# Block sums of a mixing matrix: added by VectorE and GpSimd, or by transfers in DRAM

## The chip, the cores and the metric

One core of a Trainium2 chip runs the whole program. The time is that of the device for one execution, in microseconds (us), and the median over several executions is compared. The engines that matter: TensorE (PE in the profile; PEld is its weight load) multiplies, VectorE (DVE) and GpSimd (POOL) do element-wise work, ScalarE (ACT) does activations and copies out of PSUM, SyncE (SP) only issues transfers. ScalarE and GpSimd issue transfers too. Each engine takes its instructions in order.

## The reference

The input x is 2048 x 512. It is normalised by rows (xn), and two branches are made of it:

```python
xn = _layernorm(x, axis=-1)
s = _A_ref(xn, A_wqkv, A_wo)      # attention: 32 heads of 16, 8 taps at distance 2, then @ wo
g = _silu(_B_ref(xn, B_w_in, B_w_sp, B_b_sp, B_w_out))
return x + s * g

def _B_ref(x, w_in, w_sp, b_sp, w_out):
    z = _gelu(jnp.einsum("bsd,df->bsf", x, w_in))     # 2048 x 1792
    z1 = z[..., :Fh]                                  # Fh = 896
    z2 = _layernorm(z[..., Fh:], axis=-1)
    g = jnp.einsum("ts,bsf->btf", w_sp, z2) + b_sp[None, :, None]
    return jnp.einsum("bsf,fd->bsd", z1 * g, w_out)
```

The mixing weights w_sp are 2048 x 2048 in float32.

## The kernel before

**Number format.** Every matrix operand is split into a high and a low part (`split`, lines 194 to 198: ScalarE writes the high part, VectorE subtracts it for the low part), and each product is three matmuls: high by high, high by low, low by high. `prep` (line 175) loads a block of weights into one of four raw buffers (`fetch`, line 167, on SP's queue) and splits it into one of eight weight pairs.

**Stages on TensorE, in order:** the projections q, k, v (`product`, `pair`, three groups g of 16 row tiles, written to DRAM as `qkv_d`); z1 (seven blocks f by four column groups c, lines 695 to 711, written to DRAM as `z1_d`); z2 (eight pairs of row tiles i and 8 + i, lines 780 to 801); the mixing product w_sp by z2 (`block_product`, from line 990); the projection by w_out (`proj`, line 1075); and the projection by wo (line 1124).

**The mixing by fewer products.** w_sp is cut into column halves a = 0, 1 and within each into four kinds of block: t0, t1 (rows' upper half r = 0, columns c = 0, 1) and l0, l1 (lower half). A Strassen-like scheme uses the plain blocks and four sums of them:

- number 0: t0 + t1 + l1
- number 1: t0 + t1
- number 2: l0 + t0 + t1 + l1
- number 3: t1 + l1

There are 16 sets, for a = 0, 1 and i = 0 to 7; each block of a set is 128 x 512. `added` (line 390) makes the four sums of one set in four adds. `block_sums` (line 395) loads the four blocks by two transfers of 512 KB, adds, and stores by two transfers to `sums_d`. The sets (a = 1, i = 0 to 5) run on GpSimd, loads, adds and stores alike (`pool_sums`, called at line 488 in the q, k, v stage). The eight sets of a = 0 run on VectorE during z1 (`first_sums`, lines 690 to 715; loads on SP, stores on GpSimd's queue, tiles from the eight buffers `t4` that z1's and z2's results use too). The last two sets run on VectorE during z2 (`raw_sums`, line 405, in the raw buffers of the weights, loads and stores on SP in transfers of 256 KB). `summed` (line 872) loads the sums for the later block products.

**z2 to mixing.** For each pair i VectorE takes statistics (`z2_stats`, line 738; line 745 adds epsilon), GpSimd raises to the power -0.5 (line 746), ScalarE normalises (line 754), the result is split and combined (`combine`, line 759). The first mixing products need these and the weight blocks `wsp_*`. The PSUM banks are first seeded with the biases by ScalarE (`seed`, line 842).

**Attention** is VectorE work, put between the rest: 32 steps (16 units by two), each with a product of q and k (line 573), its reduction to scores (580), a weighted product of the values (620), a fold on GpSimd (633), two more folds and a transpose (638 to 646), and a store. They are kept in one order by `line` (537), have a low priority (`LOW`) except for the score reductions, and are placed where a planner's model of the times finds VectorE free. `sums_of` lists the 32 weighted products. One hold is set by hand: the tenth weighted product (`sums_of[9]`) comes behind the split of block wsp_6 of the first mixing product (lines 864 to 867). It is an order on VectorE, not a semaphore.

Of the kernel before, what the change touches and what calls it, by code (L numbers as in the profile page):

```python
# [57 lines left out]
def kernel(  # L58
# [40 lines left out]
    y_d = dram.tile([2, ODD, P, CT], F32, name="y_d")  # L99
    sums_d = dram.tile([2, 2, HT, P, 2, CT], F32, name="sums_d")  # L100
    t_d = dram.tile([3, HT, P, F3], F32, name="t_d")
# [287 lines left out]

    def added(ts, eng):  # L390
        t0, t1, l0, l1 = ts
        for out_, p_, q_ in ((l1, t1, l1), (t1, t0, t1), (t0, t0, l1), (l0, t0, l0)):
            eng.tensor_tensor(out_, p_, q_, op=ALU.add)  # L393

    def block_sums(a, i, tile_=None, eng=nc.vector, loads=nc.sync, stores=nc.scalar, behind=None):
        top, low = [(tile_ or t4)(f"s{n}_{a}_{i}") for n in "ab"]
        for t, r in ((top, 0), (low, HT)):
            ins = loads.dma_start(t, w_sp[2 * a : 2 * a + 2, r + i].rearrange("c p t -> p c t"))
            if behind:
                tc.add_manual_dep(ins.ins, behind[0].ins.name, behind[1], reason="sums later")  # L400
        added([top[:, 0], top[:, 1], low[:, 0], low[:, 1]], eng)
        for r, t in enumerate((top, low)):
            stores.dma_start(sums_d[a, r, i], t)

    def raw_sums(a, i):
        ts = [
            fetch(w_sp[2 * a + c, r + i], CT, f"sr_{a}_{i}_{c}_{r}") for r in (0, HT) for c in range(2)
        ]
        added(ts, nc.vector)
        for n, t in enumerate(ts):  # L410
            nc.sync.dma_start(sums_d[a, n // 2, i, :, n % 2], t)

    def early_tile(name):
        return t2(name).rearrange("p (i t) -> p i t", i=2)

    def pool_sums(a, i, tile_, *behind):
        block_sums(a, i, tile_, nc.gpsimd, nc.gpsimd, nc.gpsimd, behind)

    z1_sums = [(0, i) for i in range(HT)]

# [57 lines left out]
    for j in range(11, NT):  # L478
        if j + 2 < NT:
            fetch_cols(j + 2)  # L480
        if j == NT - 3:
            rb = raws.tile([P, 512], F32, tag="raw", name="rb", bufs=RAW)
            rbv = rb.rearrange("p (j q) -> p j q", j=JC)
            pin(nc.sync.dma_start(rbv, mv_d[:JC, 1].unsqueeze(0).to_broadcast([P, JC, P])))
        turned = column_tile(j)
        if j == 12:
            for i in range(HT - 2):
                pool_sums(1, i, early_tile, turned, SYNC)
        low_x(j - 1, cols[j - 1])
        if j % 2:  # L490
            pair(0, j - 5)
# [15 lines left out]
    for g in range(1, NG):  # L507
        for j in range(OPEN if g == 1 else 0, NT, 2):
            if g == 1 and j == NT // 2:
                pins[0] = True  # L510
                wgs[2] = weights(2)
            pair(g, j)
            pins[0] = False

    for t in (1, 2):
# [173 lines left out]

    def first_sums(a, i):  # L690
        block_sums(a, i, stores=nc.gpsimd)

    first_sums(*z1_sums[0])

    for f in range(FB):
        pair_ = side_pair("w1_last") if f == FB - 1 else None
        wh, wl = prep(w_in1[:, f, :], KB * P, f"w1_{f}", pair_=pair_)
        for c in range(NC):
# [11 lines left out]
            if c % 2:  # L710
                nc.scalar.dma_start(z1_d[f, c - 1 : c + 1].rearrange("c p t -> p c t"), zp)
        if f == 2:
            first_sums(*z1_sums[FB])
        if f < FB - 1:
            first_sums(*z1_sums[f + 1])

# [21 lines left out]
    def z2_stats(i, zts):  # L738
        for j, zt in zip((i, HT + i), zts):
            st = const.tile([P, 2, 6], F32, tag="st2", name=f"zst_{j}", bufs=3)  # L740
            for h in range(2):
                nc.vector.bn_stats(st[:, h], zt[:, h * FQ : (h + 1) * FQ])  # L742
            nc.vector.bn_aggr(mvz[:, j], st)
        mean, rstd = [mvz[:, i : i + HT + 1 : HT, n] for n in range(2)]
        nc.vector.tensor_scalar(rstd, rstd, EPS, None, op0=ALU.add)
        nc.gpsimd.tensor_tensor(rstd, rstd, nhalf.to_broadcast([P, 2]), op=ALU.pow)
# [33 lines left out]
    for i in range(HT + 2):  # L780
        if i in (1, 3):
            raw_sums(1, HT - 2 + i // 2)
        if i < HT:
# [88 lines left out]
    def summed(a, half_, i):  # L872
        return lambda s: prep(sums_d[a, half_, s, :, i], CT, f"ws_{a}{half_}{i}_{s}")

# [304 lines left out]
```

## Time and profile before

| | us |
|---|---|
| median of 3 runs | 697.74 |
| lowest, highest | 696.59, 699.07 |
| the profiled execution, its time | 696.54 |
| the profiled execution, its span | 694.8 |

Line numbers such as L393 are those of the kernel before. A timeline row has the start, the length, the engine, the line, the operation, its result and operands, and in brackets the idle time before it with what ended it. A row of the busy time by stage has the stage, its length, then the busy time (and the count) of each engine, the granted TensorE clock as a share, the mean busy share of the DMA engines (its estimate can pass 1), and GB/s. A row of costs has the group, its count, its busy time, the mean of one in ns, and the idle time before it.

### The profile page before, as it was taken

The numbers are of one execution on the slowest core, as the hardware profiler recorded it, in microseconds if no ns is written. First come the engines' busy times: TensorE is split into PE (matmuls) and PEld (weight loads), VectorE is DVE, ScalarE is ACT, GpSimd is POOL, SyncE is SP. The second block draws the span as 40 slices with busy tenths as digits, with TensorE's granted clock in tenths as the row PEclk, the third lists the DMA queues.
The fourth block names the chain that finished last, engine by engine and source line by source line (L and its number), as shares of the span: only waits on it lengthen the run. The fifth ranks groups of instructions, "written<-read, shape, count | busy, mean of one in ns | idle before, by whom it ended". The sixth has DMA issues, their size and how long they took to land.

```text
span 694.8 us, 9233 instructions
## 1 busy us (share of the span) xinstructions
PE 686.6 (99%) x3084; PEld 573.0 (82%) x3084; DVE 619.4 (89%) x866; ACT 277.7 (40%) x458; POOL 215.2 (31%) x242
## 2 busy tenths in 40 slices
PE   8999999999999999998999999999999999999998
PEld 7888888888888899986888888888888888888886
DVE  6776868999989989889999998999989999989775
ACT  4342234224424256865534544442334444211531
POOL 3104837372343322124123222223111201642320
PEclk9999999999999999999999999999999999999999
DMA  8769899969999865267899768667576692655796
GB/s 270 252 193 289 288 348 384 346 204 358 407 412 340 329 231 190 80 201 231 258 403 314 284 211 298 208 232 248 183 261 206 215 342 89 221 173 190 246 330 235
DMA packets 102223, 182.36 MB, mean 262 GB/s; under 512 B 9184, under 2 KB 45280, under 8 KB 102176
## 3 DMA queue, kind: packets, MB, share of 16 engines
q1 hardware_dynamic: 56624, 102.21, 43.6%
q0 software_dynamic: 13824, 52.24, 20.9%
q10 hardware_dynamic: 31728, 27.33, 11.7%
q8 instruction: 24, 0.39, 0.2%
q14 instruction: 23, 0.19, 0.1%
HBM read 122.42 MB, written 59.32 MB: 262 GB/s over the span
## 4 chain that ended last, share of the span: by engine, by line
PE 67%; DVE 13%; DMA 12%; ACT 3%; issue 3%; POOL 1%; SPq 1%; DVEq 0%; POOLq 0%; ACTq 0%
PE g L825 35%; PE b L1067 4%; PE b L1069 4%; PE b L1068 4%; PE qkv L387 4%; PE qkv L386 4%; PE qkv L385 4%; DMA sb<-in_w_sp 3%; PE s L1069 2%; PE s L1068 2%; PE s L1067 2%; DMA sums_d<-sb 2%; DVE zst L742 2%; DMA z_d<-z1t 1%; DVE xT L280 1%
## 5 line engine op out<-in xcount | busy, mean ns | idle before, releaser
L633 POOL TENSOR_TENSOR pv<-pv 128x1024 f32<-128x1024 f32 x29 | 69.6, 2399 | 96.2 <-DVE pv L620 85.9
L573 DVE TENSOR_TENSOR pr<-k,q 128x2048 f32<-128x2048 f32 x32 | 73.6, 2299 | 2.0 <-DMA k<-qkv_d 1.9
L620 DVE TENSOR_TENSOR pv<-v,lg 128x2048 f32<-128x2048 f32 x32 | 74.6, 2331 | 0.7
L580 DVE TENSOR_REDUCE lg<-pr 128x128 f32<-128x2048 f32 x32 | 73.0, 2281 | 0.1
L647 POOL DMA_DIRECT2D o_d<-tt x32 | 18.0, 562 | 138.9 <-DVE tt L646 103.8
L433 ACT ACTIVATE stage<-qkv 128x512 f32<-128x512 f32 x40 | 23.0, 590 | 30.8 <-DMA qkv_d<-stage 17.0
L807 POOL DMA_DIRECT2D ol<-o_d x32 | 17.7, 555 | 37.7 <-DVE BIG L197 11.1
L1078 ACT ACTIVATE bt<-b 128x512 f32<-128x512 f32 x16 | 9.4, 599 | 43.5 <-PE b L1069 39.4
L709 ACT ACTIVATE z1t<-z 128x512 f32<-128x512 f32 x28 | 15.5, 597 | 26.1 <-DMA z_d<-z1t 15.3
L280 DVE TENSOR_TENSOR xT<-xT,mr 128x512 f32<-128x512 f32 x20 | 14.9, 743 | 11.9 <-DMA mr<-mv_d 6.4
L732 PE MATMUL z<-w_0h,BIG 128*128 128x512 f32 x64 | 25.0, 391 | 0.0
L731 PE MATMUL z<-w_0l,BIG 128*128 128x512 f32 x64 | 25.0, 391 | 0.0
L730 PE MATMUL z<-w_0h,BIG 128*128 128x512 f32 x64 | 24.9, 390 | 0.0
L742 DVE BATCH_NORM_STATS2 zst<-zt 128x6 f32<-128x448 f32 x32 | 19.3, 613 | 6.1 <-ACT zt L733 6.0
L754 ACT ACTIVATE zt<-zt,nmz,mvz 128x896 f32<-128x896 f32 x16 | 17.5, 1129 | 18.0 <-POOL nmz L748 18.0
L638 DVE TENSOR_TENSOR pv<-pv 128x512 f32<-128x512 f32 x32 | 22.9, 716 | 0.0
L733 ACT ACTIVATE zt<-z 128x512 f32<-128x512 f32 (+1 forms) x32 | 15.9, 536 | 15.2 <-DMA sums_d<-sa 14.0
L732 PE MATMUL z<-w_1h,BIG 128*128 128x384 f32 x64 | 21.5, 336 | 0.0
L730 PE MATMUL z<-w_1h,BIG 128*128 128x384 f32 x64 | 21.5, 335 | 0.0
L731 PE MATMUL z<-w_1l,BIG 128*128 128x384 f32 x64 | 21.4, 335 | 0.0
L393 POOL TENSOR_TENSOR sb<-sa,sb 128x512 f32<-128x512 f32 x12 | 19.7, 1644 | 5.4 <-DMA sb<-in_w_sp 5.1
L195 ACT ACTIVATE BIG<-zl 128x512 fp32r<-128x512 f32 x20 | 12.5, 630 | 21.6 <-DVE zl L895 19.8
(478 smaller groups left out, 2296.2 us busy)
## 6 DMA issues: line engine op xcount, KB each, us to landing
qkv_d<-stage ACTq DMA_DIRECT2D x24, 512.0 KB
v<-qkv_d POOLq DMA_DIRECT2D x14, 704.0 KB, 5.4
k<-qkv_d POOLq DMA_DIRECT2D x13, 704.0 KB, 6.8
sums_d<-sa POOLq DMA_DIRECT2D x14, 512.0 KB, 7.8
sums_d<-sb POOLq DMA_DIRECT2D x14, 512.0 KB, 8.0
z_d<-z1t ACTq DMA_DIRECT2D x14, 512.0 KB
zl<-z_d SPq DMA_DIRECT2D x12, 512.0 KB
tr<-t_d SPq DMA_DIRECT2D x12, 384.0 KB
```

Of the source, the lines that this page charges most:

```text
L573: line(nc.vector.tensor_tensor(pr, taps(ks[u], j0), qb.unsqueeze(1).to_broadcast([P, W, NJ * CS]), op=ALU.mult))
L580: line(nc.vector.tensor_reduce(lgs[u][:, j0 * HS : (j0 + NJ) * HS].rearrange("p i w -> p w i"), pr.rearrange("p w (i d) -> p w i d", d=DH) ...
L620: line(nc.vector.tensor_tensor(pv.rearrange("p w (i d) -> p w i d", d=DH), taps(vs[u], j0).rearrange("p w (i d) -> p w i d", d=DH), lgs[u] ...
L633: eng.tensor_tensor(pv[:, 0:4], pv[:, 0:4], pv[:, 4:8], op=ALU.add)
L730: nc.tensor.matmul(pz, xh[:, k], wh, start=k == 0, stop=False)
L731: nc.tensor.matmul(pz, xh[:, k], wl, start=False, stop=False)
L732: nc.tensor.matmul(pz, xl[:, k], wh, start=False, stop=k == KB - 1)
L742: nc.vector.bn_stats(st[:, h], zt[:, h * FQ : (h + 1) * FQ])
L825: nc.tensor.matmul(pg, z[a], w[b], start=start and i == 0, stop=stop and i == 2, skip_group_check=seeded)
L1067: nc.tensor.matmul(pp[:, cols], hi, wh, start=k == 0, stop=False)
L1068: nc.tensor.matmul(pp[:, cols], hi, wl, start=False, stop=False)
L1069: nc.tensor.matmul(pp[:, cols], lo, wh, start=False, stop=k == n - 1)
```

## The change

The 64 adds on VectorE and GpSimd, their loads, buffers and stores go. `sums_d` becomes 32 DRAM tensors of two blocks each (a, number n, pair q of sets). A generator lists 64 transfers of 512 KB from DRAM to DRAM in five rounds: 32 copies on SP's queue (`copied`) and 32 transfers on GpSimd's queue that add their source to what stands at the destination (`plus`). Each is described as 64 rows of 2048 float32. The rounds make number 3 as l1, then + t1; number 0 as t0, then + number 3; number 1 as t0, then + t1; number 2 as l0, then + number 0. `go_on(n)` issues the next n of them: one behind each of the 13 pairs of the q, k, v stage that lie in the loop over g = 1, 2, one behind each of the 28 products of z1, two at the head of each of the ten rounds of the z2 loop. These are 61 calls' worth; the last three transfers of the generator (number 2 of a = 1, pairs 1 to 3, adding) aren't asked for.

The hold on the tenth weighted product goes. The sixteenth (`sums_of[15]`) is put behind the statistics of the last z2 pair (line 745 for i = 7) instead.

```diff
-    sums_d = dram.tile([2, 2, HT, P, 2, CT], F32, name="sums_d")
+    sums_d = {
+        (a, n, q): dram.tile([2, P, CT], F32, name=f"sums_{a}_{n}_{q}")
+        for a in range(2)
+        for n in range(4)
+        for q in range(HT // 2)
+    }
...
-    def added(ts, eng):
...
-    def block_sums(a, i, tile_=None, eng=nc.vector, loads=nc.sync, stores=nc.scalar, behind=None):
...
-    def raw_sums(a, i):
...
+    def rows_of_2k(blocks_):
+        return blocks_.rearrange("s p t -> (s p t)").rearrange("(r x) -> r x", x=4 * CT)
+
+    def raw_blocks(a, n, q):
+        r, c = divmod(n, 2)
+        j = r * HT + 2 * q
+        return w_sp[2 * a + c, j : j + 2]
+
+    def copied(to, a, q, src):
+        nc.sync.dma_start(rows_of_2k(sums_d[a, to, q]), rows_of_2k(src(a, q)))
+
+    def plus(to, a, q, src):
+        nc.gpsimd.dma_start(rows_of_2k(sums_d[a, to, q]), rows_of_2k(src(a, q)), accum_op=ALU.add, max_dma_last_dim=2048)
+
+    def weight_sums():
+        t0, t1, l0, l1 = [lambda a, q, n=n: raw_blocks(a, n, q) for n in range(4)]
+        s0, s3 = [lambda a, q, n=n: sums_d[a, n, q] for n in (0, 3)]
+        rounds = (
+            ((copied, 3, l1),),
+            ((copied, 0, t0), (plus, 3, t1)),
+            ((copied, 1, t0), (plus, 0, s3)),
+            ((copied, 2, l0), (plus, 1, t1)),
+            ((plus, 2, s0),),
+        )
+        for ops in rounds:
+            for a in range(2):
+                for q in range(HT // 2):
+                    for fn, to, src in ops:
+                        yield fn, to, a, q, src
+
+    coming_sums = weight_sums()
+
+    def go_on(n):
+        for fn, *args in itertools.islice(coming_sums, n):
+            fn(*args)
...
-        turned = column_tile(j)
-        if j == 12:
-            for i in range(HT - 2):
-                pool_sums(1, i, early_tile, turned, SYNC)
+        column_tile(j)
...
             pair(g, j)
             pins[0] = False
+            go_on(1)
...
                 nc.scalar.dma_start(z1_d[f, c - 1 : c + 1].rearrange("c p t -> p c t"), zp)
-        if f == 2:
-            first_sums(*z1_sums[FB])
-        if f < FB - 1:
-            first_sums(*z1_sums[f + 1])
+            go_on(1)
...
-        nc.vector.tensor_scalar(rstd, rstd, EPS, None, op0=ALU.add)
+        known = nc.vector.tensor_scalar(rstd, rstd, EPS, None, op0=ALU.add)
+        if i == HT - 1:
+            tc.add_manual_dep(sums_of[15].ins, known.ins.name, NOSYNC, reason="gate rows ahead")
...
     for i in range(HT + 2):
-        if i in (1, 3):
-            raw_sums(1, HT - 2 + i // 2)
+        go_on(2)
...
-            pair_ = spatial.get((2 * a + c, js)) or spatial_block(2 * a + c, js)
-            if (a, c, js) == (0, 0, 6):
-                tc.add_manual_dep(
-                    sums_of[9].ins, lows[-1].ins.name, NOSYNC, reason="first weights ahead"
-                )
-            return pair_
+            return spatial.get((2 * a + c, js)) or spatial_block(2 * a + c, js)
...
     def summed(a, half_, i):
-        return lambda s: prep(sums_d[a, half_, s, :, i], CT, f"ws_{a}{half_}{i}_{s}")
+        return lambda s: prep(sums_d[a, 2 * half_ + i, s // 2][s % 2], CT, f"ws_{a}{half_}{i}_{s}")
```

More of the change, by code (lines that the diff above doesn't have):

```diff
@@ L388, in product @@
         return pq
-    def added(ts, eng):
-        t0, t1, l0, l1 = ts
-        for out_, p_, q_ in ((l1, t1, l1), (t1, t0, t1), (t0, t0, l1), (l0, t0, l0)):
-            eng.tensor_tensor(out_, p_, q_, op=ALU.add)
-    def block_sums(a, i, tile_=None, eng=nc.vector, loads=nc.sync, stores=nc.scalar, behind=None):
[L396 to L403, printed above, removed]
@@ L405, in raw_sums @@
-    def raw_sums(a, i):
[L406 to L419, printed above, removed]
+    def rows_of_2k(blocks_):
+        return blocks_.rearrange("s p t -> (s p t)").rearrange("(r x) -> r x", x=4 * CT)
@@ L688 @@
     attention()
-    def first_sums(a, i):
-        block_sums(a, i, stores=nc.gpsimd)
-    first_sums(*z1_sums[0])
     for f in range(FB):
```

## The prediction

> **What bounds the kernel now.** I read the page's busy times, then the busy time by stage, then TensorE's timeline at the few places where it stands still.
>
> ```profile
> span 694.8 us, 9233 instructions
> PE 686.6 (99%) x3084; PEld 573.0 (82%) x3084; DVE 619.4 (89%) x866; ACT 277.7 (40%) x458; POOL 215.2 (31%) x242
> 70.00:150.00 80.00, 80.00 (x354) 66.24 (x353) 67.04 (x58) 26.28 (x48) 49.91 (x46) 1.00 0.97 330
> 150.00:235.00 85.00, 85.00 (x384) 71.39 (x384) 82.19 (x105) 26.23 (x43) 32.41 (x36) 1.00 0.97 363
> 66.82 0.39 PE L386 MATMUL qkv<-wqkv_0l,BIG 128*128 128x512 f32 x1
> 67.41 0.50 PE L387 MATMUL qkv<-wqkv_0h,BIG 128*128 128x512 f32 x1 [0.20 <-DVE BIG L234]
> 314.89 0.39 PE L825 MATMUL g<-wsp_6h,BIG 128*128 128x512 f32 x1
> 317.17 0.50 PE L825 MATMUL g<-wsp_0h,BIG 128*128 128x512 f32 x1 [1.90 <-ACT g L843]
> 317.51 0.40 PE L825 MATMUL g<-wsp_0l,BIG 128*128 128x512 f32 x1
> 323.88 0.39 PE L825 MATMUL g<-wsp_3h,BIG 128*128 128x512 f32 x1
> 324.48 0.50 PE L825 MATMUL g<-wsp_7h,BIG 128*128 128x512 f32 x1 [0.21 <-ACT BIG L195]
> ```
>
> In the window rows the first number after the length is TensorE's busy time, then weight loads, VectorE, ScalarE, GpSimd, the granted clock, the DMA share and GB/s. TensorE is busy through whole stages at clock 1.00. A busy TensorE need not be at its peak, so I count starts: 354 matmuls in the 80 us of the first window are 0.226 us each (the second has narrower ones among them, so it holds more), and a step of 0.23 us is what the timeline shows wherever TensorE isn't kept waiting. Its matmuls are untouched by the diff, so the most that can be won is the time in which it does not start one at this pace. Behind the opening that is three places: 67.41 - 66.82 - 0.23 = 0.36 us, 317.17 - 314.89 - 0.23 = 2.05 us, and 324.48 - 323.88 - 0.23 = 0.37 us. The step behind a gap is long too (317.51 - 317.17 = 0.34, 0.1 over), so 0.46 + 2.15 + 0.47 = **3.1 us** in all. That is the ceiling of any gain, 0.44% of 697.74.
>
> The Trainium skill (Trainium Kernel Development and Optimization, Performance Expectations) holds matmul busy time to be a bad metric and weight-load busy time a good one; by that, 82% would leave far more room than 3 us. Here the start-to-start pace, not the 99%, closes that room.
>
> The large gap is in the passage from z2 to the mixing products. Its rows, by engine:
>
> ```profile
> 303.43 0.69 DVE L197 TENSOR_TENSOR wsp_6l<-wsp_6r,wsp_6h 128x512 fp32r<-128x512 f32 x1 [1.42 <-ACT wsp_6h L195]
> 304.04 2.29 DVE L620 TENSOR_TENSOR pv<-v,lg 128x2048 f32<-128x2048 f32 x1
> 306.24 2.28 DVE L580 TENSOR_REDUCE lg<-pr 128x128 f32<-128x2048 f32 x1
> 309.82 0.67 DVE L197 TENSOR_TENSOR wsp_7l<-wsp_7r,wsp_7h 128x512 fp32r<-128x512 f32 x1
> 310.52 0.33 SPq L169 DMA_DIRECT2D wsp_3r<-in_w_sp  x1
> 313.99 0.64 ACT L195 ACTIVATE wsp_3h<-wsp_3r 128x512 fp32r<-128x512 f32 x1 [5.03 <-DMA wsp_3r<-in_w_sp]
> 316.53 2.14 ACT L843 ACTIVATE g<-b_bh 128x512 f32<-128x512 f32 x4
> 318.58 0.16 DVE L745 TENSOR_SCALAR mvz<-mvz 128x2 f32<-128x2 f32 x1
> 318.82 1.68 POOL L746 TENSOR_TENSOR mvz<-mvz,nhalf 128x2 f32<-128x2 f32 x1 [1.83 <-DVE mvz L745]
> ```
>
> As soon as wsp_6l is split (the present hold), VectorE takes a weighted product and a score reduction of the attention, 4.4 us. Behind them wsp_7l frees its raw buffer late, the load of wsp_3r starts late, ScalarE stands 5.03 us before wsp_3h, and the bias seeds, queued behind it, come at 316.53: TensorE waits for them. The last z2 statistics (318.58) are also behind attention pieces, and feed the gap at 324.48.
>
> **The change, part by part.** First the adds. The columns are VectorE and GpSimd time on line 393, with counts:
>
> ```profile
> 54.00:155.00 101.00, 0.00 (x0) 37.62 (x24) 1.00 0.92 312
> 155.00:235.00 80.00, 18.78 (x28) 0.00 (x0) 1.00 1.01 380
> 235.00:325.00 90.00, 8.56 (x13) 0.00 (x0) 1.00 0.57 194
> L500 DVE TENSOR_TENSOR xs<-xs,rb 128x512 f32<-128x512 f32 x4 | 6.1, 1532 | 0.1
> 80.46 0.69 DVE L500 TENSOR_TENSOR xs<-xs,rb 128x512 f32<-128x512 f32 x1
> ```
>
> VectorE loses 40 adds, 18.78 + 8.56 = 27.3 us (an add that lies across 235 is counted in both windows); GpSimd loses 24, 37.6 us. While GpSimd adds, VectorE's own operations stretch: L500 takes 0.69 us in a pause of the adds at 80.46, but 1.53 on average. That line alone gives back 6.1 - 4 x 0.69 = 3.3 us, and the late L234 behind the gap at 67.41 lies in the same stretch; without those adds its gap of 0.46 us should go. None of the 27.3 + 3.3 = 30.6 us is on TensorE's path by itself. It is worth what it lets attention do earlier.
>
> **The moved hold.** Before, the tenth weighted product waits for the split of wsp_6; afterwards the sixteenth waits for L745 of the last z2 pair.
>
> ```profile
> 0.00:152.40 152.40, 8.24 (x3) 1.00 0.88 291
> 152.40:235.00 82.60, 13.72 (x6) 1.00 0.98 368
> 295.00:317.00 22.00, 2.29 (x1) 1.00 0.62 192
> L620 DVE TENSOR_TENSOR pv<-v,lg 128x2048 f32<-128x2048 f32 x32 | 74.6, 2331 | 0.7
> L573 DVE TENSOR_TENSOR pr<-k,q 128x2048 f32<-128x2048 f32 x32 | 73.6, 2299 | 2.0 <-DMA k<-qkv_d 1.9
> L580 DVE TENSOR_REDUCE lg<-pr 128x128 f32<-128x2048 f32 x32 | 73.0, 2281 | 0.1
> L638 DVE TENSOR_TENSOR pv<-pv 128x512 f32<-128x512 f32 x32 | 22.9, 716 | 0.0
> ```
>
> The first three rows count L620: nine products before 235, the tenth at 304. Up to L745 five more are now allowed. One step costs VectorE at least 2.33 + 2.30 + 2.28 + 0.72 = 7.6 us, five 38 us: the 30.6 us freed pay four of them, and VectorE idles 80 - 67.04 + 85 - 82.19 = 15.8 us between 70 and 235 besides. So attention can come near the new hold, and what is left of it then cannot step between wsp_6l and wsp_7l. Behind the held product stand all later attention operations of VectorE, the GpSimd folds and the stores of its results; nobody on TensorE's path needs them before the last projection, and 32 - 15 = 17 products then have the time that 32 - 10 = 22 have now. If the 4.4 us at 304 are gone, wsp_3r is issued some 4 us earlier and the seeds come before 314.89: 2.15 us won. What is late next is the last z2 pair itself (the 0.47 us at 324.48), which I leave standing.
>
> **The transfers.** Of the 64 steps of the generator, the loops ask for 5 + 8 in the qkv stage, 28 in z1, 20 in z2: 61, so 32 copies and 29 adding transfers of 512 KB. The sites put 13 before z1, 28 in z1 and 20 in z2.
>
> ```profile
> 170.00:190.00 20.00, 20.00 (x90) 16.57 (x89) 19.89 (x30) 6.66 (x10) 6.58 (x10) 1.00 1.04 411
> 150.00:235.00 85.00, 7.57 (x14) 1.00 0.97 363
> L398 SPq DMA_DIRECT2D sa<-in_w_sp x8: 367/460/853, 158.1 to 221.0; - x8
> sums_d<-sa POOLq DMA_DIRECT2D x14, 512.0 KB, 7.8
> sa<-in_w_sp POOLq DMA_DIRECT2D x6, 512.0 KB, 7.1
> ```
>
> The third row is line 403, the stores of sums. Before, 28 loads and 28 stores of 512 KB and 8 + 8 of half that carry the sums: 64 transfers' worth, so at one unit per transfer nothing is added. No row shows an adding transfer. Bounds: one unit (a plain transfer; larger pieces could bring it a little below, which nothing here is bound by) and three (two sources read and one result written, one after the other, each as dear as the 7.1 us load or the 7.8 us store). I take two: load and store differ little, so I count passes on the heavier side, and there it reads twice. The tight stage is 150 to 235: 363 GB/s x 85 us = 30.9 MB, of which 16 loads (two groups of eight) and 14 stores are 15.7 MB. Afterwards 14 copies and 14 adds take 7.3 + 7.3x, so the stage asks for 29.8 MB at x = 1, 37.1 at two, 44.5 at three, against 34.9 MB at the 411 GB/s of the best row. At two, 2.2 MB or 5.4 us slip into z2, where the DMA share was 0.57 (the row of 235 to 325). Cover: the weights for z1 and most of z2 are loaded ahead, so I cost it at nothing. If the cover is gone, see the second rival.
>
> The Trainium skill (Collectives: The Full Stack, The bandwidth ceiling) says that a reducing transfer runs at about half the rate of a copy because it reads two sources. By it x is two and the stage is over-subscribed; no run here shows it yet.
>
> Issues: SP loses 16 + 8 loads and 8 stores and gains 32 copies, no difference. GpSimd loses 28 stores, 12 loads and 37.6 us of adds, and gains 29 issues. Four may stand before its L746 at 318.82; it had idled 1.83 us there. An adding transfer waits in GpSimd's queue for the copy or sum that it builds on, issued eight or more sites earlier; a site of z1 is 12 x 0.226 = 2.7 us, so 22 us against the 7.8 of a landing: no wait. The sums are first loaded for the fifth block product, 4 x 96 x 0.226 = 87 us into the mixing.
>
> **The sum.** 0.46 + 2.15 = 2.6 us off the profiled run's 696.54 (span 694.8 and 1.74 around it): 693.9. The median of the runs shown is 1.20 higher, so **695.1**.
>
> **Rivals.** (1) *The gap stays.* The order is planned from modelled times; score reductions and weight splits may meet in another place, or VectorE reaches only the thirteenth product by 304, so that the new hold never binds and the change doesn't do what it says. For it: every freed microsecond is needed. Against: the extra idle time. Only 0.46 goes: 697.3.
>
> (2) *Transfers choke z1: slower.*
>
> ```profile
> 141.60:213.00 71.40, 13.71 (x22) 1.00 0.93 352
> 141.60:215.00 73.40, 41.75 (x108) 20.27 (x108) 1.00 0.94 354
> 211.53 0.42 ACT L606 ACTIVATE lg<-lg 128x256 f32<-128x256 f32 x1 [4.27 <-DVE lg L601]
> ```
>
> By 215 TensorE has filled 108 / 4 = 27 banks of z1, while ScalarE's 22 entries on L709 (two are table loads) emptied 20: seven of eight banks are full, 12 x 0.226 = 2.7 us short of a stall, with ScalarE held by attention. If keys and values come 5.4 us late (x = 2), VectorE and ScalarE wait in order and TensorE stalls 2.7 us; with the gap at 317 left, 697.3 + 2.7 = 700.0. It decides from x = (34.9 - 15.2 - 7.3) / 7.3 = 1.7. At x = 3 it is 23 us late: up to 20 us, less what the freed buffers add to the cover (fully behind, eight banks are 21.7). Against: the sums' own buffers, for which ScalarE waited, are free. On the skill's rule this is the case to fear.
>
> (3) *VectorE is overdrawn: slower.* If five steps are planned ahead of L745 and the idle 15.8 us cannot be used, L745 slips by 38 - 30.6 = 7.4 us, and the gap at 324.48 grows by that: 697.3 + 7.4 = 704.7. It decides once more than 30.6 / 7.6 = 4 steps go ahead without idle time.
>
> **How the numbers follow.** Forecast 0.45; (1) 0.32; (2) 0.15; (3) 0.08. Faster means over 0.3% (2.1 us, about what a measurement of this kernel can tell from no change), same is within it: 0.45, 0.32, 0.23. Low end: the ceiling 697.74 - 3.1, less the 1.15 us between the median and the lowest run: 693.5. High end: (2) at two, with 1 us for the spread of the runs, 701; what x = 3 would cost and (3) are left out, some 0.15 together.
>
> **What would show it.** Right: steps of 0.23 us at 67 and across the passage; ten to fifteen L620 before the last L745; L500 near 0.69. Wrong: a TensorE gap in z1 or z2 with a DMA or key load behind it, adding transfers landing far above 8 us, or a new gap at the first mixing products.

## The result, and the profile after

| | before | after |
|---|---|---|
| median, us | 697.69 (4 runs, 696.59 to 699.07) | 891.85 (4 runs, 888.49 to 899.07) |
| ratio | 1 | 1.2795 (95% interval 1.2712 to 1.2878) |
| profiled execution, its time | 696.54 | 899.07 |
| q, k, v end | 141.4 | 332.3 |
| z1 lasts | 75.9 | 75.9 |
| z2 lasts | 77.1 | 77.1 |
| mixing lasts | 275.4 | 287.1 |

The kernel became 28% slower, where 0.4% faster was forecast. The stages are read from TensorE's timeline in the profiled execution, from the first to the last product of each. In the tables medians are of all executions; the ratios leave out one slow execution each of two runs below, late (708.42) and nosums_old (3232.39). Nearly everything was lost ahead of z1: 332.3 - 141.4 = 190.9 us. The mixing lost 287.1 - 275.4 = 11.7 us more. z1 and z2, where the second rival looked for trouble, are as they were.

The page of the changed kernel, with the span in 40 slices of 22.4 us; a digit is the busy share in tenths:

```profile
span 897.3 us, 9099 instructions
...
PE   7104703000399999999998899998999999999998
...
DMA  9994988555568767765052669876865677536294
```

TensorE does next to nothing in slices 3, 6 and 8 to 10, and in the last three no engine is busy for more than a tenth or two: this is a wait, not work. The busy time by stage, columns as in the prediction, has the same stretch and the quiet stages behind it:

```profile
150.00:240.00 90.00, 1.51 (x4) 1.22 (x5) 3.60 (x7) 0.83 (x2) 14.33 (x16) 0.50 0.61 96
332.00:408.00 76.00, 76.00 (x337) 62.93 (x336) 73.83 (x88) 30.82 (x47) 28.07 (x27) 1.00 0.69 230
408.00:485.00 77.00, 77.00 (x383) 69.08 (x382) 71.34 (x120) 41.60 (x62) 31.79 (x30) 1.00 0.32 105
```

In the first row's 90 us TensorE started four matmuls, with the clock granted at 0.50, and VectorE is busy for 3.60 us, so it isn't VectorE that holds GpSimd up there. z1 (the second row) has a DMA share of 0.69 and z2 (the third) 0.32. Where the same sums are made in these stages, in the run held below, the shares are 0.97 and 0.82. GpSimd's timeline and the end of TensorE's wait say what happened instead:

```profile
187.86 0.89 POOL L407 DMA_DIRECT2D sums<-in_w_sp  x1 [5.20 <-issue]
193.86 0.90 POOL L407 DMA_DIRECT2D sums<-in_w_sp  x1 [5.11 <-issue]
...
234.49 0.89 POOL L407 DMA_DIRECT2D sums<-sums  x1 [4.89 <-issue]
235.08 1.22 POOL L272 TENSOR_TENSOR mvx<-mvx,nhalf 128x3 f32<-128x3 f32 x1
238.49 0.80 PE L392 MATMUL qkv<-wqkv_0h,BIG 128*128 128x512 f32 x1 [91.83 <-DVE BIG L239]
```

L407 is the adding transfer, L272 GpSimd's power in the row statistics of x, on which the products of q, k and v wait (power, a store and a load of the result, the normalised block, its split, then the product: 238.49 - 235.08 = 3.4 us). One power of three values stands behind all 29 adding transfers, and TensorE waits 91.83 us for it. What the adding transfers have done by then:

```profile
L407 POOL DMA_DIRECT2D sums<-in_w_sp x16: 886/899/1151, 12.5 to 193.9; - x16
L407 POOL DMA_DIRECT2D sums<-sums x13: 891/899/954, 113.5 to 234.5; - x13
  issue: 152.4, 24
DMA to landing us min/median/max: 5.1/5.7/25.2
```

The first two rows give minimum, median and maximum length in ns and the first and last start; the third is GpSimd's idle time before them, the fourth the time from issue to landing. All 29 were issued between 12.5 and 234.5 us, the last 98 us before z1 began. And before 24 of them GpSimd stood still for nothing that the profile shows, 152.4 us in all, 4.4 to 5.8 us for each where one follows another from 145 us on. By the landings in the trace one transfer is under way at a time: nearly each goes out 0.3 us behind the landing of the one before, and while the copies are moved that takes longest (the one issued at 45.84 landed at 70.99, the next went out at 71.31). On SP the copies (L404) stand among the opening loads in the same way:

```profile
3.52 0.91 SPq L207 DMA_DIRECT2D x<-in_x  x2
4.47 2.23 SPq L404 DMA_DIRECT2D sums<-in_w_sp  x3
7.60 0.34 SPq L207 DMA_DIRECT2D x<-in_x  x1
8.27 2.08 SPq L404 DMA_DIRECT2D sums<-in_w_sp  x3
```

### The profile page after: what moved, and what is told of

It is laid out like the page before. It is cut to its first block, busy times and chain, and to the rows that moved or that the text cites. A ratio compares the mean times of both kernels' runs of the same rounds, so it can differ in the third digit from the quotient of the medians.

```text
span 897.3 us, 9099 instructions
## 1 busy us (share of the span) xinstructions
PE 699.6 (78%) x3084; PEld 580.7 (65%) x3084; DVE 579.0 (65%) x826; ACT 289.5 (32%) x464; POOL 191.2 (21%) x207
## 2 busy tenths in 40 slices
DMA packets 98719, 180.79 MB, mean 201 GB/s; under 512 B 9008, under 2 KB 45104, under 8 KB 98160
## 4 chain that ended last, share of the span: by engine, by line
PE 57%; issue 17%; DMA 12%; DVE 6%; POOL 4%; ACT 2%; SPq 1%; DVEq 0%; POOLq 0%; ACTq 0%
PE g L826 22%; DMA sums<-in_w_sp 4%; PE qkv L392 4%; PE qkv L390 3%; PE qkv L391 3%; DMA x<-in_x 3%; PE b L1064 3%; PE z L708 3%; PE z L706 3%; PE b L1065 3%; PE b L1063 3%; PE z L707 3%; POOL sums L407 2%; DMA qkv_d<-stage 2%; PE s L1064 2%
## 5 line engine op out<-in xcount | busy, mean ns | idle before, releaser
L392 PE MATMUL qkv<-wqkv_0h,BIG 128*128 128x512 f32 x43 | 17.6, 408 | 108.7 <-DVE BIG L239 108.7
L392 PEld LDWEIGHTS qkv<-wqkv_0h,BIG 128*128 128x128 f32 x43 | 8.3, 193 | 111.5 <-DVE BIG L239 109.9
L628 DVE TENSOR_TENSOR pv<-v,lg 128x2048 f32<-128x2048 f32 x32 | 73.3, 2290 | 0.9 <-DMA v<-qkv_d 0.2
L288 ACT ACTIVATE BIG<-xT 128x512 fp32r<-128x512 f32 x10 | 6.3, 632 | 122.3 <-DVE xT L285 121.8
L233 PE MATMUL xt<-ident,x 128*128 128x128 f32 x24 | 4.7, 328 | 49.1 <-DVE mvx L218 49.1
L407 POOL DMA_DIRECT2D sums<-in_w_sp x16 | 14.7, 922 | 106.1 <-issue 95.3
L233 PEld LDWEIGHTS xt<-ident,x 128*128 128x128 f32 x24 | 3.3, 169 | 50.9 <-DVE mvx L218 50.4
L407 POOL DMA_DIRECT2D sums<-sums x13 | 11.7, 900 | 78.5 <-issue 57.1
L390 PE MATMUL qkv<-wqkv_0h,BIG 128*128 128x512 f32 x43 | 16.8, 406 | 14.2 <-ACT BIG L288 14.2
L732 PE MATMUL z<-w_0h,BIG 128*128 128x512 f32 x64 | 25.0, 391 | 0.0
```

The costliest lines, as they stand in the source:

```text
L390: nc.tensor.matmul(pq, xh[:, k], wh, start=k == 0, stop=False)
L392: nc.tensor.matmul(pq, xl[:, k], wh, start=False, stop=k == KB - 1)
L407: nc.gpsimd.dma_start(rows_of_2k(sums_d[a, to, q]), rows_of_2k(src(a, q)), accum_op=ALU.add, max_dma_last_dim=2048)
L628: line(nc.vector.tensor_tensor(pv.rearrange("p w (i d) -> p w i d", d=DH), taps(vs[u], j0).rearrange("p w (i d) -> p w i d", d=DH), lgs[u] ...
```

## The experiments

Theory 1: the order was the fault. A copy of the changed kernel waits for nothing and an adding transfer only for what it builds on, so the planner put them near the front of SP's and GpSimd's queues; where the calls are written had no say. Rival A: an adding transfer stops GpSimd wherever it stands, and a better order would only move the loss. Rival B: the DMA engines run out. Theory 2, for the mixing: the moved hold costs what is lost there, whatever is done with the sums. The medians, each beside runs of the kernel before on the same chip (a run of one execution has no interval):

| run | us | before | ratio, interval |
|---|---|---|---|
| held | 754.97 | 695.06 | 1.0866 (1.0801 to 1.0931) |
| held_big | 720.50 | 695.04 | 1.0366 (1.0345 to 1.0386) |
| held_big_old | 708.66 | 695.42 | 1.0201 (1.0172 to 1.0230) |
| late | 697.58 | 695.04 | 1.0025 (1.0001 to 1.0049) |
| nosums_old | 693.43 | 695.42 | 0.9972 (0.9963 to 0.9982) |
| nosums_new | 704.92 | 695.42 | 1.0160 (1.0124 to 1.0196) |
| moved | 709.60 | 695.06 | 1.0205 (1.0176 to 1.0235) |
| plain, big, copies_front (one execution each) | 796.78, 833.25, 745.28 | | |
| probe, probe4k (one execution each) | 714.82, 696.84 | | |

### held: each transfer behind ScalarE's step at its place

```diff
...
 def go_on(n):
     for fn, *args in itertools.islice(coming_sums, n):
-        fn(*args)
+        ins = fn(*args)
+        tc.add_manual_dep(ins.ins, marks[-1].ins.name, NOSYNC, reason="sums in place")
```

`marks` lists ScalarE's evictions of q, k, v, z1 and z2 as they are written. The order is the planner's only; it is no semaphore.

> The changed kernel with one thing added: each of the 61 transfers is ordered behind the latest ScalarE operation at the place where it is written (in the plan alone, no semaphore). Theory 1 (the planner put the transfers, which wait for nothing, at the front of both queues, and the row statistics on GpSimd stood behind them): TensorE's 191 us lost before z1 come back, 695 to 715 us. Rival A (an adding transfer holds GpSimd's queue for 5.8 us wherever it stands): 29 x 5.8 = 168 us of GpSimd in z1 and z2, so attention and z2 wait, 740 us or more. Rival B (the traffic of the transfers itself slows the loads): the loss moves into z1 and z2, 720 us or more.

754.97 us: 136.9 of the 194 lost came back, which fits the 740 or more of rival A and the 720 or more of rival B, and not the 695 to 715 of theory 1. q, k, v end at 141.3, as before the change: all 191 us there were the order. But z2 now takes 111.5 us. Two of the waits of GpSimd and ScalarE in this run (total, times, longest):

```profile
POOL sums L407 <- issue: 112.2, 21, 9.0
ACT zt L759 <- POOL nmz L753: 72.2, 9, 34.1
```

The stops at the adding transfers came along to their new places, and ScalarE's normalising of z2 waits for GpSimd's statistics behind them, once 34.1 us. So theory 1 and rival A both hold in part: the order lost the most, and the stops lose time where something that TensorE needs stands behind them. Seven of them, 42.8 us, stand in z1, and z1 takes no longer than before (76 us).

### big and plain: the changed kernel with other pieces

```diff
-    ..., accum_op=ALU.add, max_dma_last_dim=2048)
+    ..., accum_op=ALU.add, max_dma_last_dim=8192)      # big
+    ..., max_dma_last_dim=2048)                        # plain
```

> The changed kernel with the adding transfers cut into pieces of 8 KB in place of 2 KB (4 per DMA engine in place of 16), everything else and the order the same. If GpSimd stops because the pieces of one adding transfer fill the queue's store of descriptors, several fit now: the distance from one to the next falls from 5.8 us to under 2, and the time to 720 to 790. If the adding itself holds the queue, or the engine waits for each to land, the distance stays at 5 to 6 us and the time at 880 to 900.

> The changed kernel with the 29 adding transfers made plain copies of the same pieces of 2 KB on the same queue in the same order (the sums are left out, the output is not the reference's). If adding is what holds GpSimd's queue, the distance falls to about 1 us and the time to 700 to 760. If the number of pieces holds it, a copy (one read and one write entry per piece) lets perhaps two or three stand at a time: 2 to 4 us apart, 760 to 830. If the place in the order alone mattered, nothing changes: 880 to 900.

With pieces of 8 KB (64 a transfer in place of 256) the time is 833.25, which is in neither range of its expectation; with no adding it is 796.78, within 760 to 830. Neither gets near 700, since the order is untouched; q, k, v end at 265.4 and 227.8. Plain doesn't tell adding from the number of pieces, though: its trace has 98719 - 95007 = 3712 DMA records fewer than the changed kernel's, 128 for each of the 29 transfers, so the copies went in 128 pieces of 4 KB and not in 256. In big GpSimd's stops have shrunk from 152.4 to 31.6 us (11 times) and the row statistics are earlier, but something else is late:

```profile
PE qkv L390 <- ACT BIG L288: 79.2, 1, 79.2
ACT stage L443 <- DMA qkv_d<-stage: 73.3, 1, 73.3
```

ScalarE, in order, stands 73.3 us before an eviction because the stores that should free its buffer do not land, while transfers of the sums fill the DMA engines. So transfers at the front do harm beside GpSimd's stops too: rival B is true of the opening, and copies_front below shows it with no stop at all.

### moved: only the hold, in the kernel before

```diff
+        known = nc.vector.tensor_scalar(rstd, rstd, EPS, None, op0=ALU.add)
+        if i == HT - 1:
+            tc.add_manual_dep(sums_of[15].ins, known.ins.name, NOSYNC, reason="gate rows ahead")
...
-            if (a, c, js) == (0, 0, 6):
-                tc.add_manual_dep(
-                    sums_of[9].ins, lows[-1].ins.name, NOSYNC, reason="first weights ahead"
-                )
...
```

> The kernel before with the other half of the change alone: the hold goes from the tenth weighted product to the sixteenth, behind the last z2 statistics; sums as before. If the hold costs nothing by itself: 695 to 700 us. If it is what makes the new gaps between z2 and the mixing (11.7 us more in the mixing stage of the changed kernel): 703 to 712.

709.60, 14.5 us slower than before, with the sums still made by the engines. The mixing takes 287.7 us against 275.4, which is the loss of the changed kernel there (287.1). What the third rival feared is seen here: the last z2 statistics (L745 before) slip from 318.6 to 333.9. nosums_new shows what happens with VectorE freed of the adds.

### held_big and held_big_old: pieces and hold on top of held

held_big is held with pieces of 8 KB; held_big_old has the hold of before as well.

> held_big_old with the changed kernel's hold in place of the one of before; it tells the size of the pieces apart from the hold. Pieces (against the run 'held', 755.0): z2 from 111.5 us to 85 or less. Hold: 10 to 14 us more than held_big_old's 708.7, in z2's end and the first mixing products, as in 'moved' and 'nosums_new': 717 to 724. Rival (the two add to each other, since attention steps among the z2 statistics also wait for keys and values): 728 or more.

> The changed kernel with three things put right one upon the other: each transfer is kept behind ScalarE's step at the place where it is written (as in the run 'held'), the adding transfers move pieces of 8 KB in place of 2 KB, and the hold on the attention is the one of before (the tenth weighted product behind wsp_6). Theory (GpSimd stands at each adding transfer until the DMA engines have taken enough of its pieces, and 256 small pieces make that 5 us and more where 64 large ones do not; the moved hold costs some 12 us on top): q, k, v end at 141 as before, z2 back to about 80 us from 111.5, mixing back to about 277 from 296: 697 to 712. Rival (the adding transfer itself holds GpSimd, whatever its pieces): z2 stays above 100 us and the time is 735 to 745, 12 less than 'held' for the hold alone. Second rival (the DMA engines' capacity is what runs out, with transfers where they were forecast to stand): TensorE gaps in z1 and z2 end with loads, 715 to 730.

720.50 and 708.66. The pieces are worth 754.97 - 720.50 = 34.5 us, most of it in z2 (111.5 to 84.5); the hold 720.50 - 708.66 = 11.8 us. In held_big_old GpSimd stands at L407 for 1.3 us in all. What is left are two gaps of TensorE, 5.3 us up to 237.9, in the first part of z2, and 6.5 us up to 329.7, in the first mixing products. ScalarE's longest single wait names the first:

```profile
ACT z1t L715 <- DMA z_d<-z1t: 42.6, 4, 16.9
```

and the busy time by stage the cause:

```profile
141.00:217.00 76.00, 76.00 (x337) 62.94 (x336) 57.03 (x64) 24.37 (x38) 33.18 (x35) 1.00 1.01 326
```

The DMA engines are full through z1 (1.01), and the stores of z1 hold ScalarE up to 16.9 us. In the passage it is the loads of the mixing weights, 5.41 us before wsp_0h. That is the second rival's mechanism, one stage further on than forecast.

### copies_front: only the adding transfers kept at their places

```diff
             ins = fn(*args)
-            tc.add_manual_dep(ins.ins, marks[-1].ins.name, NOSYNC, reason="sums in place")
+            if fn is plus:
+                tc.add_manual_dep(ins.ins, marks[-1].ins.name, NOSYNC, reason="sums in place")
```

> As held_big_old, but only the adding transfers are kept at their places; the 32 copies may go to the front of SP's queue as in the changed kernel. Theory A (the late opening is GpSimd's queue alone, the copies do no harm): q, k, v end at 141 to 143, the time is that of held_big_old within 3 us. Theory B (copies in front of the opening's own loads and small stores take DMA time that these need): the q, k, v stage is longer by 32 copies' DMA time or a part of it, 20 to 60 us, with gaps that end with loads of x, of weights or with the stores of stage.

745.28. q, k, v end at 192.1, 50.7 us later than in held_big_old (z2 and the mixing win back 16.8, since the copies are out of their way). TensorE's largest wait:

```profile
PE qkv L390 <- ACT BIG L288: 20.6, 1, 20.6
```

And the opening from 40 to 75 us, first in this run and then in held_big_old:

```profile
40.00:75.00 35.00, 20.81 (x84) 16.75 (x84) 6.59 (x16) 7.38 (x13) 1.88 (x2) 0.79 0.96 325
```

```profile
40.00:75.00 35.00, 34.37 (x152) 28.02 (x151) 22.94 (x39) 13.05 (x24) 1.22 (x1) 1.00 0.60 180
```

With GpSimd out of it (the first L407 comes at 176.4), 32 copies issued from 4.5 to 70.4 us, of which nothing is needed for another 100 us, fill the DMA engines (0.96 against 0.60), and the opening's own loads and stores wait among them.

### nosums_old and nosums_new: nothing is made, with either hold

```diff
-        return lambda s: prep(sums_d[a, 2 * half_ + i, s // 2][s % 2], CT, f"ws_{a}{half_}{i}_{s}")
+        return lambda s: prep(raw_blocks(a, 2 * half_ + i, s // 2)[s % 2], CT, f"ws_{a}{half_}{i}_{s}")
```

All calls of `go_on` go too; nosums_old has the hold of before besides.

> No sums are made at all: no transfers for them, no adds; the later block products read raw blocks of w_sp in their place. The hold is the one of before. What is left is what the freed VectorE and GpSimd are worth by themselves, with nothing to pay. The forecast's reason (freed engines are worth 0.46 us at 67 at once, and up to 3.1 us in all): 693 to 696. Rival (freeing engines lets the planner bring attention forward to worse places): 698 to 706.

> As nosums_old, no sums made, but with the changed kernel's hold (the sixteenth weighted product behind the last z2 statistics). The forecast's reason (five more weighted products are paid by the 30.6 us that VectorE is freed of and by its idle time, and the gap at 317 closes): 693 to 695, no later than nosums_old. Rival (VectorE is overdrawn or its attention pieces stand among the z2 statistics, whatever has been freed): 702 to 709, with gaps of 5 us and more in the first mixing products, as in the run 'moved'.

nosums_old takes 693.43, 2.0 us less than before; its span is 691.6 against 694.8, 3.2 us, where the ceiling was put at 3.1. From 30 us on no two starts of TensorE are more than 0.24 us apart: all three gaps of the forecast are closed, the one at 317 too, with the old hold. L507 (L500 before) takes 0.69 us four times.

nosums_new takes 704.92, 11.5 us more for the hold alone. Its profiled execution is the fastest of its four, 9.4 us over that of nosums_old, and 8.1 of these are two gaps of TensorE: 5.4 us up to 302.69 and 3.1 us up to 321.18, each less a step of 0.23. The rows that follow lead to the first; the second, before which ScalarE's bias seeds are late, was not followed further. VectorE's timeline in nosums_new, and then that of GpSimd, ScalarE and TensorE:

```profile
289.31 0.10 DVE L743 TENSOR_SCALAR mvz<-mvz 128x2 f32<-128x2 f32 x1
289.34 0.54 DVE L767 TENSOR_TENSOR zt<-zt,zt 128x384 f32<-128x384 f32 x1
...
290.74 2.27 DVE L580 TENSOR_TENSOR pr<-k,q 128x2048 f32<-128x2048 f32 x1
...
295.69 0.67 DVE L202 TENSOR_TENSOR wsp_4l<-wsp_4r,wsp_4h 128x512 fp32r<-128x512 f32 x1
```

```profile
289.50 7.43 POOL L746 TENSOR_TENSOR mvz<-mvz,nhalf 128x2 f32<-128x2 f32 x1 [8.35 <-DVE mvz L743]
297.33 2.16 ACT L754 ACTIVATE zt<-zt,nmz,mvz 128x896 f32<-128x896 f32 x2 [6.37 <-POOL nmz L748]
302.69 0.79 PE L977 MATMUL g<-BIG 128*128 128x512 f32 x1 [5.00 <-ACT zt L731]
```

In nosums_old the same power of two numbers per row stands as

```profile
289.87 1.07 POOL L744 TENSOR_TENSOR mvz<-mvz,nhalf 128x2 f32<-128x2 f32 x1 [8.08 <-DVE mvz L743]
```

VectorE gives the statistics (L743) and goes on from 289.34 to 295.69 + 0.67 = 296.36 with elementwise operations on two operands, back to back, an attention product among them. GpSimd's power, 0.70 to 1.68 us in nosums_old, lasts until 289.50 + 7.43 = 296.93, 0.57 us behind the last of them. ScalarE's normalising waits 6.37 us for it, z2's last evictions stand behind that, and TensorE waits 5.00 us. The pair is late besides: it is the sixth of eight here, at 289.3, where nosums_old gave the sixth at 280.0 and the seventh at 289.6. The changed kernel has the same picture:

```profile
481.20 7.43 POOL L748 TENSOR_TENSOR mvz<-mvz,nhalf 128x2 f32<-128x2 f32 x1 [8.36 <-DVE mvz L745]
494.39 0.80 PE L980 MATMUL g<-BIG 128*128 128x512 f32 x1 [5.02 <-ACT zt L733]
```

### probe and probe4k: the adding transfer by itself

```diff
+        if i == 3:
+            moves(nc.gpsimd, 0, 2048, 6, accum_op=ALU.add)
+        if i == 5:
+            moves(nc.gpsimd, 1, 8192, 6, accum_op=ALU.add)
+        if i == 7:
+            moves(nc.gpsimd, 2, 2048, 6)
```

This stands in z2 of nosums_old; `moves` issues so many transfers of 512 KB in pieces of the given size, and twelve copies on SP's queue stand ahead of them. probe4k has two groups of 4096 in their place.

> nosums_old with three groups of six transfers of 512 KB on GpSimd's queue in z2, where the DMA engines are nearly idle (0.23): adding in 2 KB pieces, adding in 8 KB pieces, plain in 2 KB pieces; their results are used by nothing. Theory (GpSimd stands because the list of pieces that it may have outstanding is full): the first two or three of the 2 KB adds are issued about 1 us apart, then each stands until pieces have been moved, 3 to 6 us; the 8 KB adds go out 1 us apart or little more; the plain ones stand less than the adding ones, since their pieces move faster (some 90 ns against 211). Rival (GpSimd spends the time writing 256 pieces): 2 KB transfers are 3 to 6 us apart from the first on, adding and plain alike, and 8 KB ones a quarter of that. The whole: 693 to 696.

> nosums_old with two groups of six adding transfers of 512 KB in pieces of 4 KB on GpSimd's queue in z2; their results are used by nothing. In the run 'probe' one adding transfer of 256 pieces made the next one stand, three plain ones of 128 pieces went out at once and the fourth stood, six adding ones of 64 pieces went out at once: so a queue that holds at least 3 x 128 = 384 and fewer than 2 x 256 = 512 pieces. Theory (that limit, whatever the kind): the first three of each group 0.8 to 1 us apart, the fourth stands 2 us or more, then one per 3 to 5 us, the time of 128 pieces. Rival (the stop is a price of each adding transfer by the number of its pieces): the second already stands about 2.5 us, half of what 256 pieces cost, and all later ones alike.

GpSimd's timeline in probe: three of the 2 KB adds and what follows the last, the six 8 KB adds in one row, and the plain ones:

```profile
241.43 1.02 POOL L407 DMA_DIRECT2D sums<-in_w_sp  x1
247.47 0.90 POOL L407 DMA_DIRECT2D sums<-in_w_sp  x1 [5.02 <-issue]
255.31 0.90 POOL L407 DMA_DIRECT2D sums<-in_w_sp  x1 [6.94 <-issue]
...
273.48 1.06 POOL L736 TENSOR_TENSOR mvz<-mvz,nhalf 128x2 f32<-128x2 f32 x1
...
283.05 4.94 POOL L407 DMA_DIRECT2D sums<-in_w_sp  x6
...
307.14 1.81 POOL L407 DMA_DIRECT2D sums<-in_w_sp  x3
311.39 0.56 POOL L407 DMA_DIRECT2D sums<-in_w_sp  x1 [2.44 <-issue]
```

And in probe4k:

```profile
230.23 2.68 POOL L407 DMA_DIRECT2D sums<-in_w_sp  x3
239.11 0.81 POOL L407 DMA_DIRECT2D sums<-in_w_sp  x1 [6.20 <-issue]
...
264.10 2.60 POOL L407 DMA_DIRECT2D sums<-in_w_sp  x3
269.84 0.82 POOL L407 DMA_DIRECT2D sums<-in_w_sp  x1 [3.14 <-issue]
```

The expectation that the first two or three 2 KB adds go out at once was wrong: the second already stands. The 8 KB adds go out 0.8 us apart, as expected. The plain transfers were moved in pieces of 4 KB, 128 each, by the records of the DMA engines, so that they are no test of plain pieces of 2 KB: three went at once and the fourth stood. That led to probe4k's forecast from a limit of between 3 x 128 = 384 and 2 x 256 = 512 outstanding pieces, and both its groups do as forecast: three at once, the fourth stands. The rival, a price on each transfer, falls: the second 4 KB add doesn't stand. The landings in the traces say what ends a stop. With 256 pieces a transfer goes out some 0.3 us behind the landing of the one before it (247.13, then 247.47), with 128 behind that of the third before it (238.80, then 239.11), and in big, where the queue filled, with 64 behind that of the seventh before it (72.80, then 73.07). So the room comes back when a whole transfer has landed, and seven of 64 pieces still fit: 448 and more, fewer than 512. The whole of probe missed its 693 to 696 by 19 us: the six 2 KB adds kept the queue from 241 to 273, and the statistics behind them (L736 at 273.48) were late for z2 and the mixing. In probe4k the queue is free again after some 15 and 11 us, and the time is 696.84, 3.4 us over nosums_old on another chip.

### late: the same transfers where the DMA engines have room

```diff
...
-            ((copied, 2, l0), (plus, 1, t1)),
+            ((plus, 1, t1),),
+            ((copied, 2, l0),),
             ((plus, 2, s0),),
...
-            go_on(1)
+            if c == 1 or c == 3 and f in (1, 3, 5, 6):
+                go_on(1)
...
-        go_on(2)
+        go_on(3 if i < HT else 0)
...
-            steps=([T1[2 * a]], [], [T1[2 * a + 1]], []),
+            steps=([T1[2 * a], two], [], [T1[2 * a + 1], two], []),
...
-        block_product(a, "m4", at(1, 0), plain(a, 1, 1), odd(1))
+        block_product(a, "m4", at(1, 0), plain(a, 1, 1), odd(1), steps=([two], [], [two], []))
```

`two` issues the next two transfers, kept behind the split of a weight block. All 64 are issued.

> As held_big_old (transfers kept at their places, 8 KB pieces, the hold of before), all 64 transfers, and spread by where the run nosums_old leaves the DMA engines free: 13 in q, k, v, 11 in z1, 24 in z2, the 16 of number 2 during the fourth to sixth kind of block product, where nothing needs them yet. Theory (what is left in held_big_old, 5.3 us at the opening of z2 and 6.5 us in the first mixing products, is DMA time in z1 and at the passage alone): both gaps go, 693 to 697. Rival (an adding transfer costs GpSimd or the mixing's loads time wherever it stands): gaps of some us in z2 or among the later block products, 699 to 710.

697.58, with a ratio of 1.0025 (1.0001 to 1.0049), just above the 693 to 697 of its expectation. z1 lasts 75.9 us, z2 77.1, and the mixing 273.7 in the profiled execution; both gaps of held_big_old are gone, with the DMA engines nearly full in z1 and z2:

```profile
141.00:217.00 76.00, 76.00 (x337) 62.91 (x336) 60.35 (x71) 27.41 (x43) 30.06 (x30) 1.00 0.90 284
217.00:294.00 77.00, 77.00 (x384) 69.21 (x383) 47.99 (x100) 45.84 (x73) 20.06 (x34) 1.00 0.95 231
```

It is 11.1 us better than held_big_old, and no better than before. The executions compared lie between 693.24 and 700.30, those of nosums_old between 693.15 and 693.59; why they spread more here stays open. No version with the sums made by transfers beat the kernel before, and nosums_old, which makes none, puts what is left to win by making them otherwise, with the rest as it is, at about 2.0 us.

## Why the prediction was wrong, point by point

The loss of 194 us comes apart in one chain of medians: 891.85, with the order put right 754.97 (136.9 us), with larger pieces 720.50 (34.5), with the old hold 708.66 (11.8), with the transfers spread 697.58 (11.1). Each step is uncertain by some 2 us, since the runs come from different chips, on which the kernel before takes 695.04 to 697.69. The shares hold in this order alone: larger pieces put in first, with the order as it was, won 891.85 - 833.25 = 58.6 us (big).

**The step that failed first: "The sites put 13 before z1, 28 in z1 and 20 in z2."** This is where the calls are written, not where the planner issues them; the trace has all 61 before z1. The kernel before had its hold against this: `pool_sums(1, i, early_tile, turned, SYNC)` makes GpSimd's loads of the sums wait for a step of the opening, with the reason "sums later". The prediction treated the removal of these calls as a removal of work alone, though the diff shows that a wait goes with them, and a transfer from DRAM to DRAM doesn't even wait for a tile. By held, putting the transfers back to these places won 136.9 us, and no rival had it.

**"An adding transfer waits in GpSimd's queue for the copy or sum that it builds on ...: no wait."** Waits on data are not what holds it in the changed kernel; it waits for room, which comes back when an earlier transfer has landed: 24 stops, 152.4 us there and 112.2 us in held. At the front the copies make it worse, since a landing took up to 25.2 us among them, against the 7.8 that the prediction reckoned with. The queue's work was counted as 29 issues and weighed against 37.6 us of adds that go. A sign of it stood in the kernel before, in GpSimd's timeline:

```profile
62.31 0.73 POOL L398 DMA_DIRECT2D sb<-in_w_sp  x1 [5.02 <-issue]
```

The fourth transfer of 512 KB in a row stood 5.02 us for no wait that the trace names, until 0.3 us behind the landing of the first (61.99). By the records of the DMA engines these loads went in pieces of 4 KB, so this is the fourth of 128 that probe4k found. By held and held_big the stops are worth 34.5 us once the order is right.

**The moved hold.** Its reach was right: in nosums_new 15 weighted products come ahead of the last statistics, 11 of them before z2, as in the changed kernel. That they cost TensorE nothing was wrong, and "cannot step between wsp_6l and wsp_7l" did not help: four products fall into z2 itself, delay the statistics of the sixth pair by 9 us, and one of GpSimd's powers lasts 7.43 us beside VectorE's work. The third rival had the right cause, attention ahead of the statistics, and gave it 0.08, but it put the delay at the last pair, which in nosums_new is no later (311.4 against 312.1). That it said 704.7 and nosums_new took 704.92 is luck: its 7.4 us are the overdraft of VectorE, and the 7.43 us here are a single power beside it. It had said that it decides once the idle time of VectorE can't be used. That time was used: in z2 VectorE is busy 71.74 of 77 us in nosums_new and 47.81 in nosums_old. The error was to take a busy but not overdrawn VectorE for harmless; the statistics pass from VectorE to GpSimd to ScalarE, and come late once VectorE has next to no pauses.

**The price of an adding transfer.** Two was taken, with one and three as bounds. From 150 to 240 in the changed kernel there is hardly anything but 2 KB adds: share 0.61 for 96 GB/s, 96 / 0.61 = 157 GB/s for full engines, against 411 / 1.04 = 395 in the best row of before: 2.5, in terms of what was written. So the size was near. The rule of the Trainium skill (Collectives: The Full Stack, The bandwidth ceiling), half the rate of a copy, is borne out in kind and is low for pieces of 2 KB.

**The second rival** (transfers choke z1) did not decide the result, since the transfers weren't there. Once they are put there (held_big_old) its mechanism is seen: full engines and ScalarE held in z1, there by its stores and not by late keys and values. TensorE loses nothing in z1 itself, but 5.3 us in z2, where 2.7 us in z1 were forecast, and 6.5 us in the passage.

**What stood.** TensorE's pace as the limit, the ceiling (3.1 us; 3.2 measured in nosums_old's span), the gap at 67 going with GpSimd's adds, L500 at 0.69 us. The gap at 317 closed with no change of the hold, in nosums_old and also in late, where the DMA engines are nearly full: freeing VectorE seems to be enough. So the 2.6 us of gains came out near in size (2.0 by the medians), but 2.15 of them not by the moved hold to which they were put down, and the change lost some 70 times as much by what it queued in front of others.

## What to carry to other kernels

When a change takes out an instruction that waited, ask what its wait kept back: where a planner orders by dependencies, as here, a transfer with nothing to wait for goes to the front of its queue, and everything behind it on that engine pays. Count an engine that issues transfers by the room in its queue, not by the length of the issue: many small pieces stop it, and here GpSimd got through six transfers of 64 pieces at 0.8 us each, where those of 256 took it 6 us each. And off the critical path is not enough: here a long stretch of two-operand work on VectorE held a tiny step of GpSimd for which TensorE was waiting.

## What the runs showed of the hardware that was not expected

- The rows of probe and probe4k fit a GpSimd queue with room for 384 to 511 outstanding pieces: a second transfer of 256 pieces stands 5 to 7 us, a fourth of 128 stands 2 to 6 us, six of 64 don't stand. In big seven of 64 were outstanding and the eighth stood 5.36 us, which narrows it to 448 to 511. A stop ends about 0.3 us after an earlier transfer has landed as a whole. Of 128 pieces it is the same for adding and plain ones.
- A GpSimd power of 128 x 2 numbers lasted 7.43 us instead of 1.07, and ended 0.57 us behind a row of VectorE operations on two operands. In moved one lasted 4.56 us and ended 0.58 us behind the last such operation, while a reduction with one operand was still running. That the row is the cause is read from these ends; no run took the row away alone. The Trainium skill (SBUF — State Buffer, SBUF: two separate sides) says that GpSimd and a VectorE operation with two inputs in SBUF share a pair of ports under an exclusive lock, held for one whole instruction. The trace agrees in kind; but here the power did not end between the ten instructions of the row.
- The copies of 512 KB on SP's queue, far ahead of their use, cost the opening 50.7 us (copies_front), with the DMA engines at 0.96 from 40 to 75 us where they are at 0.60 without them.
